# Decoding of w_out: sums of two or three blocks in one instruction, fewer steps per slot of attention, and another layout of the second stage's memory

## The chip, the cores and the metric

One core of a Trainium2 chip. Times are device microseconds of one execution. TensorE (PE) multiplies, VectorE (DVE) and ScalarE (ACT) work on elements, SyncE (SP) issues most transfers (DMAs); each engine works off its own instructions in program order and waits by semaphores. GpSimd (POOL) only clears a few constants.

## The reference

```python
def _attn_ref(q, k, v):                      # (8, 12, 448, 64)
    scores = scale * np.matmul(q, k.transpose(0, 1, 3, 2)) - np.log(S)
    attn = 1.0 / (1.0 + np.exp(-scores))
    return np.matmul(attn, v)

x = attn_out.transpose(0, 2, 1, 3).reshape(3584, 768)
h = x @ w_in                                 # w_in (768, 2048), float64 in memory
g = np.maximum(0.01 * h, h)
return g @ w_out                             # w_out (2048, 768), float64 in memory
```

The inputs q, k and v are float32; w_in and w_out come as 64-bit floats and are turned into 32-bit ones in the kernel.

## The kernel before

Every operand of a product is split into a rounded high part (made by ScalarE or VectorE) and a low part (x minus high, made by VectorE). Three matmuls (high x high, high x low, low x high) stand for one.

**Attention** runs in 24 rounds over pairs of heads, two pairs a round. A round has five slots: scores of the first pair, scores of the second, attention times v for the first and for the second, and a short ending. A slot's chores come ahead of its matmuls: copies of the results of the round before (`keep`, on VectorE for one of the two), the low parts of the next pairs' q and k (tile `qks`, slots 3 and 4), loads. **The first stage**, h = x w_in, is four passes of 56 slots (Strassen's scheme with 7 products, 18 matmuls a product, two slots each); it writes g, and sums of blocks of g, to memory. Low parts of w_in (tile `w`) are made three slots ahead of their use. **The second stage** is 52 products on two accumulators, lanes A and B, each product with one of 24 forms (sums of blocks) of w_out and a sum of blocks of g. Results collect in output tiles `o`.

**Decoding.** A generator, `prep`, decodes the weights step by step on VectorE, in 8 blocks of w_in, then 8 of w_out; a block comes in 4 pieces of 5 instructions (tile `wd`), and each `yield` ends a step. For a block of w_in, `firsts` makes four sums and stores; 9 empty steps (`WAIT`) follow. For a block of w_out, `second` makes sums of the 8 sub-blocks of 192 columns after the list `STEPS`: the first ones into a new tile `ws` (s0 to s7) and partly in place, then it stores both tiles ("store", to the memory tile `t`), then waits 9 empty steps, then makes more sums in place in `wd` (d0 to d7) and stores them. The sums behind the wait overwrite what is being stored, so the first of them also waits for that transfer itself.

In attention `prepare(pace, time)` is called after each slot. It adds the slot's pace to a credit and takes steps, one credit each, while the time counted for VectorE's instructions (0.14 us and a column's time for each) is below the slot's time:

```python
credit += pace
while credit >= 1 and queue < time - LESS:
    next(preps, None)
    credit -= 1
queue = max(0.0, queue - time)
```

In the first three passes of the first stage `fill` takes up to 4 steps a slot while the counted time is below 1.6 us of a slot's 1.8. `now` counts slots (3 before round 0); `ALONE` = 100 is the count from which decoded pieces are loaded ahead less far.

**Memory.** The tile pools on the left side lie one behind the other: `ring` (weights of the first stage, v), `stage` (their raw form), `l` tiles, then, after attention, `st` (results of the first stage) and `m` tiles; `l` and `m` hold the first stage's last operands. After the first stage the same addresses take `t2b` (weights of the second stage), `outp` (8 output tiles), `op` (8 more tiles for operands of the second stage). A tile's first use waits for the last use of what lay there. PSUM's 8 banks take `px` (banks 0 to 3) and `pz` (4 to 7) in the first stage, lane A (0 to 2), lane B (3 to 5) and two single banks `one` in the second; the last bank tiles of the first stage's last products are `px` (2, 3) and `pz` (6, 7).

All helper-issued instructions carry line 127 in the profile; read it by tile names.

Of the kernel before, what the change touches and what calls it, by code (L numbers as in the profile page):

```python
# [14 lines left out]
ALU = mybir.AluOpType  # L15
PSUM = bass.MemoryType.PSUM

P = 128
# [6 lines left out]
RING, STAGE = 4, 4  # L25
ST = 7
AHEAD, FAR, SPARE = 5, 6, 1
GG, OO, WW = 7, 8, (3, 3)
READY, LEAD = 2, 2

PACES = 5.5, 6.5, 5.5, 3.7, 2.7
TIMES = 1.92, 1.92, 2.33, 2.33, 1.66
PRODUCT, LESS, MOST = 1.8, 0.2, 4
WAIT = 9
ALONE = 100
LATER = 4
IDLE = 7
# [9 lines left out]


PRODUCTS = (
# [13 lines left out]
FORMS = 24  # L63
BLOCKS = "00", "01", "10", "11", "20", "21", "30", "31"
STEPS = (
# [7 lines left out]


def part(i):
# [14 lines left out]
def attn_ffn_kernel(ctx: ExitStack, tc: tile.TileContext, qk, v, w_in, w_out, out):  # L90
# [54 lines left out]
    def sub(to, x, y):  # L145
        vec(out=to, in0=x, in1=y, op=ALU.subtract)
# [21 lines left out]
        now += 1  # L168

    left, right = ExitStack(), ExitStack()  # L170
    ring = left.enter_context(tc.tile_pool(name="ring", bufs=RING))
    stage = left.enter_context(tc.tile_pool(name="stage", bufs=STAGE))

    prepared = set()

    class Weights:
# [17 lines left out]
    class Wide:  # L194
# [18 lines left out]
        def of(self, part, e, m):  # L213
            return self.t[:, part, e, m * P:m * P + P]
# [58 lines left out]
    def banks(name, sizes, stack=ps):  # L273

        pool = stack.enter_context(tc.tile_pool(name=name, bufs=1, space=PSUM, reuse_waits="tile"))

        def psum(tag, name):
            bufs, n = sizes[tag]
            return pool.tile([P, n, 512] if n > 1 else [P, 512], F32, tag=tag, name=name, bufs=bufs)

        return psum
# [50 lines left out]
    def firsts(u, dec):  # L332
# [7 lines left out]
            yield  # L340
        dma(out=to[:, 3:], in_=sums)

    def second(u, dec):


        n = len(BLOCKS)
        size = wide // 2
        e, at = u // 2, u % 2 * size
        both = {"d": dec.rearrange("p a b -> p (a b)").rearrange("p (n m) -> p n m", n=n),
                "s": block(F32, (n, size), f"ws1_{u}")}  # L350

        def of(x):
            return both[x[0]][:, int(x[1:])]

        for what, *x in STEPS:
            if what == "wait":
                yield from (None for _ in range(WAIT))
            elif what == "store":
                side, i, n, form = x
                dma(out=t2d[:, form:form + n, e, at:at + size], in_=both[side][:, i:i + n])  # L360
            else:
                to, a, x, b, y = x
                if a == b == -1:
                    vec_st(out=of(to), in0=of(x), scalar=-1.0, in1=of(y), op0=ALU.mult, op1=ALU.subtract)
                elif b == 1:
                    (add if a == 1 else sub)(of(to), of(y), of(x))
                else:
                    sub(of(to), of(x), of(y))
                yield

    def prep():

        n = 4
        pieces = [(m, k) for m in range(len(todo)) for k in range(n)]
        raws = []

        def load():
            at = len(raws)  # L380
            if at == len(pieces):
                return
            m, k = pieces[at]
            w, u = todo[m]
            size = 4 * HW // n
            pool = (stage, "stage", 2 * HW, STAGE) if at % 2 and now < ALONE else (pp, "wr", 2 * HW, 3)
            raw = block(I32, (size, 2), f"wr{w}_{u}_{k}", pool)
            dma(out=raw.rearrange("p m t -> p (m t)"), in_=(w_in, w_out)[w][u][:, k * size:(k + 1) * size].bitcast(I32))
            raws.append(raw)

        for _ in range(3):
            load()
        yield
        for at, (m, k) in enumerate(pieces):
            w, u = todo[m]
            if k == 0:
                dec = block(F32, (4, HW), f"wd{w}_{u}")
            raw = raws[at]
            size = 4 * HW // n
            low, high = raw[:, :, 0], raw[:, :, 1]  # L400
            tf = dec.rearrange("p b m -> p (b m)")[:, k * size:(k + 1) * size]
            t = tf.bitcast(I32)
            vec_s(out=t, in0=high, scalar1=0x7FFFFFFF, scalar2=None, op0=ALU.bitwise_and)
            yield
            vec_s(out=tf, in0=tf, scalar1=W_LEAST, scalar2=W_MOST, op0=ALU.max, op1=ALU.min)
            yield
            vec_s(out=t, in0=t, scalar1=5, scalar2=2, op0=ALU.logical_shift_left, op1=ALU.logical_shift_right)
            yield
            vec_st(out=t, in0=high, scalar=-0x40000000, in1=t, op0=ALU.bitwise_and, op1=ALU.bitwise_or)
            yield  # L410
            vec_st(out=t, in0=low, scalar=29, in1=t, op0=ALU.logical_shift_right, op1=ALU.bitwise_or)
            yield
            while len(raws) < min(at + 1 + (5 if now < ALONE else 3), len(pieces)):
                load()
            yield
            if k < n - 1:
                continue
            if w == 1:
                yield from second(u, dec)
            else:  # L420
                yield from firsts(u, dec)
            prepared.add((w, u))
            yield from (None for _ in range(WAIT))

    preps = prep()
    credit = 0.0
# [566 lines left out]

    assert {(1, u) for u in range(NU)} <= prepared
    t2b = ctx.enter_context(tc.tile_pool(name="t2b", bufs=WW[1], reuse_waits="tile"))
    outp = ctx.enter_context(tc.tile_pool(name="outp", bufs=OO, reuse_waits="tile"))
    shift(ctx, "pad3", 64)
    op = ctx.enter_context(tc.tile_pool(name="op", bufs=1, reuse_waits="tile"))
    spare.extend((op, f"o{n}") for n in range(8))
    cycle = [t2a] * WW[0] + [t2b] * WW[1]  # L1000
    weights += [Wide(k, cycle[k % len(cycle)]) for k in range(WW[0], total)]
    psum = banks("ps_o", dict(A=(1, 3), B=(1, 3), one=(2, 1)))
    NM = NC // 2
    ends = max(i for i, x in enumerate(PRODUCTS) if x[2] and x[1] == PRODUCTS[-1][1])
    outs, accs = {}, {}
# [30 lines left out]
    for k in range(total):  # L1036
# [3 lines left out]
        def work():  # L1040
# [13 lines left out]
                    x.low()  # L1054
            if begins:
                if p == NQ // 2 - 1 and i == ends:
                    t, one = psum(lane, f"acc_{lane}{k}"), psum("one", f"acc_one{k}")
                    accs[lane] = [t[:, 0, :S], t[:, 1, :S], one[:, :S]], [(slice(0, 2), t[:, :2, :S]), (slice(2, 3), one[:, None, :S])]
                else:
                    t = psum(lane, f"acc_{lane}{k}")  # L1060
                    accs[lane] = [t[:, m, :S] for m in range(3)], [(slice(0, 3), t[:, :, :S])]
# [67 lines left out]
```

## Time and profile before

| | |
|---|---|
| median of 3 runs | 1067.89 us (1066.1 to 1068.75) |
| the profiled execution | 1067.47 us, span 1065.7 us |
| attention, first stage, second stage | 0 to 277.8, to 681.5, to 1065.7 us of the span |
| busy: PE, DVE, ACT | 98%, 79%, 55% |
| mean granted TensorE clock | 0.990 |
| bytes moved | 300.63 MB, mean 282 GB/s |

The times of the engines overlap; the span is set by whichever work ends last. A row such as "PE sc <- DVE qks: 10.7, 3, 4.4" says that TensorE, about to write tile sc, waited for VectorE's writing of qks 10.7 us in all, 3 times, 4.4 at the longest. In rows of a group, "busy, mean ns" stands before the second bar and idle time of the engine just before, with its releaser, behind it. In a timeline the columns are start and length in us, engine, operation, tiles, and in brackets the idle time before it.

### The profile page before, as it was taken

Reading aid. Unit: us, or ns where it says so; the run is one execution under the profiler, and the core shown is the slowest. Engines: PE = TensorE matmul, PEld = TensorE weight load, DVE = VectorE, ACT = ScalarE, POOL = GpSimd, SP = SyncE. Lnnn points to the kernel's source line nnn. Section 1 sums busy time; section 2 is a strip of 40 time slices with the busy share of each in tenths; the row PEclk is TensorE's granted clock in tenths of the full one; section 3 lists DMA queues with packets and bytes.
Section 4 is the critical chain, followed back from the end, with each engine's and each line's share of the span. In section 5 each row is a group of like instructions: output and inputs, shape, how many; then the busy total and the mean of one; then the engine's idle time right before and its main releaser. Section 6 shows DMA issues by size and latency. Waiting matters only on the chain.

```text
span 1065.7 us, 15110 instructions
## 1 busy us (share of the span) xinstructions
PE 1039.8 (98%) x5738; PEld 868.3 (81%) x5738; DVE 845.8 (79%) x1024; ACT 585.0 (55%) x610; POOL 0.3 (0%) x5
## 2 busy tenths in 40 slices
PE   9999998888999999999999999999999999999997
PEld 5545554444799999999999999889999999999997
DVE  4889997667887879878865566599998888899883
ACT  6778786666554654555556545465444526444430
POOL 0000000000000000000000000000000000000000
PEclk9999999899899999999999999999999999999999
DMA  7998877778688798898986788898668698666923
GB/s 274 316 342 289 288 284 265 252 241 297 222 304 303 245 308 285 285 335 293 377 293 208 230 298 293 333 421 343 230 248 323 253 396 329 256 238 245 319 93 129
DMA packets 113336, 300.63 MB, mean 282 GB/s; under 512 B 9200, under 2 KB 51312, under 8 KB 113264
## 3 DMA queue, kind: packets, MB, share of 16 engines
q1 hardware_dynamic: 111248, 295.19, 77.7%
q10 hardware_dynamic: 2016, 4.47, 1.1%
q8 instruction: 45, 0.74, 0.3%
q14 instruction: 27, 0.22, 0.1%
HBM read 202.77 MB, written 96.86 MB: 281 GB/s over the span
## 4 chain that ended last, share of the span: by engine, by line
PE 88%; DMA 5%; DVE 4%; issue 1%; ACT 1%; SPq 0%; ACTq 0%; DVEq 0%
PE px_h L127 22%; PE acc_B L127 17%; PE acc_A L127 16%; PE pz_h L127 11%; PE pv L127 9%; PE sc L127 8%; PE py_h L127 5%; DMA t<-wd 2%; DVE wd L127 2%; DMA w<-t 1%; DVE ws L127 1%; DVE qks L127 1%; DMA wx<-t 1%; DMA wr<-in_w_out 1%; DVE x L127 0%
## 5 line engine op out<-in xcount | busy, mean ns | idle before, releaser
L127 PE MATMUL px_h<-hi,w 128*128 128x448 f32 x768 | 223.1, 361 | 0.0
L127 PE MATMUL acc_A<-gh,w 128*128 128x448 f32 x528 | 152.6, 363 | 1.0 <-ACT c_h L127 1.0
L127 PEld LDWEIGHTS px_h<-hi,w 128*128 128x128 f32 x768 | 143.9, 187 | 11.4 <-issue 0.7
L127 DVE TENSOR_TENSOR w<-wx,w 128x768 fp32r<-128x768 f32 x112 | 106.8, 954 | 53.2 <-ACT w L127 53.2
L127 PE MATMUL px_h<-lo,w 128*128 128x448 f32 x384 | 139.4, 363 | 0.0
L127 ACT ACTIVATE s<-sc 128x896 f32<-128x896 f32 x144 | 121.0, 932 | 29.9 <-PE sc L127 29.6
L127 PE MATMUL acc_B<-gh,w 128*128 128x448 f32 x424 | 123.0, 363 | 2.5 <-ACT o L127 1.5
L127 PE MATMUL sc<-qks 64*128 64x448 f32 (+1 forms) x876 | 105.7, 392 | 16.1 <-DVE qks L127 10.7
L127 PEld LDWEIGHTS sc<-qks 64*128 64x128 f32 x876 | 85.8, 202 | 43.5 <-issue 16.9
L127 PE MATMUL pv<-s,v 128*64 128x448 f32 x576 | 114.7, 547 | 0.0
L127 PE MATMUL pz_h<-hi,w 128*128 128x448 f32 x384 | 112.8, 362 | 0.0
L127 PEld LDWEIGHTS acc_A<-gh,w 128*128 128x128 f32 x528 | 99.1, 188 | 7.8 <-ACT c_h L127 1.4
L127 ACT ACTIVATE c_h<-c_h 128x896 f32<-128x896 f32 x48 | 45.8, 954 | 86.9 <-DVE c_h L127 86.9
L127 PEld LDWEIGHTS pv<-s,v 128*64 128x64 f32 x576 | 39.3, 138 | 64.9 <-issue 54.5
L127 ACT CAST w<-wx 128x768 fp32r<-128x768 f32 x112 | 91.3, 832 | 0.1
L127 DVE TENSOR_TENSOR w<-w 128x1536 fp32r<-128x1536 f32 x52 | 91.0, 1751 | 0.0
L127 PEld LDWEIGHTS acc_B<-gh,w 128*128 128x128 f32 x424 | 79.5, 188 | 8.7 <-ACT o L127 1.9
L127 PE MATMUL acc_B<-g,w 128*128 128x448 f32 x332 | 86.0, 361 | 0.0
L127 ACT CAST w<-w 128x1536 fp32r<-128x1536 f32 x52 | 76.9, 1478 | 0.7 <-DMA w<-t 0.7
L127 PEld LDWEIGHTS pz_h<-hi,w 128*128 128x128 f32 x384 | 71.9, 187 | 5.7 <-DVE w L127 0.3
L127 PEld LDWEIGHTS px_h<-lo,w 128*128 128x128 f32 x384 | 72.1, 188 | 3.8
L127 DVE SCALAR_TENSOR_TENSOR wd<-wr,wd 128x384 int32<-128x384 int32 x128 | 71.4, 558 | 3.5
(98 smaller groups left out, 1582.8 us busy)
## 6 DMA issues: line engine op xcount, KB each, us to landing
wx<-t SPq DMA_DIRECT2D x112, 384.0 KB, 4.9
w<-t SPq DMA_DIRECT2D x52, 768.0 KB, 4.4
g<-g SPq DMA_DIRECT2D x34, 896.0 KB, 7.2
g<-c_h SPq DMA_DIRECT2D x60, 448.0 KB, 4.5
g<-s SPq DMA_DIRECT2D x48, 448.0 KB, 5.5
qk<-in_qk SPq DMA_DIRECT2D x46, 448.0 KB, 5.4
g1s<-g SPq DMA_DIRECT2D x18, 896.0 KB, 6.6
wr<-in_w_in SPq DMA_DIRECT2D x32, 384.0 KB, 5.8
```

What stands on the lines that cost most here:

```text
L127: return lambda *args, **kw: tc.keep_in_program_order(issue(*args, **kw))
```

## The change

The steps granted per slot of attention go from 23.9 to 18.0 a round. The sums of w_out are written over runs of blocks with a start and a step, so that one instruction makes one, two or three of them: 12 instructions a block of w_out instead of 18, by another order of the sub-blocks and of the 24 forms; the forms are the same sums of blocks otherwise, and the list of products changes in the forms' numbers alone. From slot count 100 on, the empty wait is 4 steps instead of 9, and the empty step behind each piece goes. On the left side `stage` comes ahead of `ring` and `op` ahead of `outp`: t2b's first tile then lies over `stage`, six of the eight `op` tiles over `l` and two over the first four `st` tiles, the first two `outp` tiles over the last three `st` tiles and the others over `m`. In PSUM the lanes lie at: one0 in bank 0, B in 1 to 3, A in 4 to 6, one1 in 7. The last product's three columns go to one0, one1 and the first bank of B, three tiles, where before the first two shared B's tile.

```diff
-PACES = 5.5, 6.5, 5.5, 3.7, 2.7
+PACES = 4, 5, 4.2, 2.8, 2
...
-WAIT = 9
+WAIT, REST = 9, 4
...
 STEPS = (
-    ("sum", "s0", 1, "d1", -1, "d7"), ("sum", "s1", -1, "d2", 1, "d4"), ("sum", "s2", -1, "d2", -1, "d3"),
...
-    ("sum", "d3", 1, "d5", -1, "d6"), ("sum", "d1", -1, "d2", 1, "d1"), ("store", "d", 0, 8, 16))
+    ("sum", 3, "sub", ("s", 0, 1), ("d", 0, 1), ("d", 2, 1)),
+    ("sum", 1, "neg", ("s", 3, 1), ("d", 3, 1), ("d", 6, 1)),
+    ("sum", 2, "sub", ("s", 4, 1), ("d", 6, 0), ("s", 1, -1)),
+    ("sum", 1, "sub", ("s", 6, 1), ("s", 4, 1), ("d", 4, 1)),
+    ("sum", 1, "sub", ("s", 7, 1), ("s", 0, 1), ("s", 1, 1)),
+    ("sum", 1, "sub", ("d", 3, 1), ("d", 3, 1), ("d", 5, 1)),
+    ("sum", 1, "neg", ("d", 2, 1), ("d", 7, 1), ("d", 2, 1)), ("store", "s", 0, 8, 0), ("store", "d", 0, 8, 8),
+    ("wait",), ("sum", 1, "add", ("d", 4, 1), ("d", 2, 1), ("d", 4, 1)),
+    ("sum", 2, "neg", ("d", 7, -6), ("d", 3, -2), ("d", 7, -3)),
+    ("sum", 2, "add", ("d", 2, 1), ("d", 2, 1), ("d", 0, 6)),
+    ("sum", 1, "neg", ("d", 5, 1), ("d", 2, 1), ("d", 5, 1)),
+    ("sum", 2, "sub", ("d", 6, -6), ("d", 4, -4), ("d", 7, -4)), ("store", "d", 0, 8, 16))
...
+    stage = left.enter_context(tc.tile_pool(name="stage", bufs=STAGE))
     ring = left.enter_context(tc.tile_pool(name="ring", bufs=RING))
-    stage = left.enter_context(tc.tile_pool(name="stage", bufs=STAGE))
...
+    def rest():
+        return (None for _ in range(WAIT if now < ALONE else REST))
...
             if what == "wait":
-                yield from (None for _ in range(WAIT))
+                yield from rest()
...
-            yield
+            if now < ALONE:
+                yield
...
             prepared.add((w, u))
-            yield from (None for _ in range(WAIT))
+            yield from rest()
...
-    outp = ctx.enter_context(tc.tile_pool(name="outp", bufs=OO, reuse_waits="tile"))
     shift(ctx, "pad3", 64)
     op = ctx.enter_context(tc.tile_pool(name="op", bufs=1, reuse_waits="tile"))
+    outp = ctx.enter_context(tc.tile_pool(name="outp", bufs=OO, reuse_waits="tile"))
...
-    psum = banks("ps_o", dict(A=(1, 3), B=(1, 3), one=(2, 1)))
+    psum = banks("ps_o", dict(one0=(1, 1), B=(1, 3), A=(1, 3), one1=(1, 1)))
+    for x in ("one0", "B", "A", "one1"):
+        psum(x, f"first_{x}")
...
-                    t, one = psum(lane, f"acc_{lane}{k}"), psum("one", f"acc_one{k}")
-                    accs[lane] = [t[:, 0, :S], t[:, 1, :S], one[:, :S]], [(slice(0, 2), t[:, :2, :S]), (slice(2, 3), one[:, None, :S])]
+                    three = [psum(x, f"acc_{x}{k}") for x in ("one0", "one1", lane)]
+                    three[2] = three[2][:, 0]
+                    accs[lane] = [x[:, :S] for x in three], [(slice(m, m + 1), x[:, None, :S]) for m, x in enumerate(three)]
```

More of the change, by code (lines that the diff above doesn't have):

```diff
@@ L49 @@
 PRODUCTS = (
[9 rows of a table removed]
[9 rows of a table added]
     (0, "A", False, ("+<1", "-1s2"), ("-010", "+110")), (6, "B", False, ("+1s1",), ("-110!",)),
[3 rows of a table removed]
[3 rows of a table added]
 FORMS = 24
-BLOCKS = "00", "01", "10", "11", "20", "21", "30", "31"
+BLOCKS = "01", "20", "31", "10", "21", "00", "11", "30"
 STEPS = (
[7 rows of a table removed]
[12 rows of a table added]
 def part(i):
@@ L350, in second, with of @@
                 "s": block(F32, (n, size), f"ws1_{u}")}
-        def of(x):
-            return both[x[0]][:, int(x[1:])]
+        def of(n, side, at, step):
+            x = both[side]
+            if step == 0:
+                return x[:, at:at + 1].broadcast_to((P, n, size))
+            end = at + (n - 1) * step + (1 if step > 0 else -1)
+            return x[:, at:end if end >= 0 else None:step]
         for what, *x in STEPS:
             if what == "wait":
-                yield from (None for _ in range(WAIT))
+                yield from rest()
             elif what == "store":
@@ L361, in second @@
             else:
[L362 to L366, printed above, removed]
+                n, fn, *x = x
+                to, x, y = (of(n, *z) for z in x)
+                if fn == "neg":
+                    vec_st(out=to, in0=x, scalar=-1.0, in1=y, op0=ALU.mult, op1=ALU.subtract)
                 else:
-                    sub(of(to), of(x), of(y))
+                    (add if fn == "add" else sub)(to, x, y)
                 yield
```

29 rows, old and new, of tables (PRODUCTS, STEPS) are left out of this document.

## The prediction

> **What bounds the kernel now.** I read the page first, then who waited for whom on TensorE and VectorE, then busy time by stretch, then the timeline at each long wait.
>
> ```profile
> span 1065.7 us, 15110 instructions
> ...
> PE 1039.8 (98%) x5738; PEld 868.3 (81%) x5738; DVE 845.8 (79%) x1024; ACT 585.0 (55%) x610; POOL 0.3 (0%) x5
> ```
>
> TensorE is busy 98% of the span, so a change that leaves its matmuls alone can win the 26 us in which it stands still, and time in which its clock is low. TensorE's waits:
>
> ```profile
> PE sc L127 <- DVE qks L127: 10.7, 3, 4.4
> PE sc L127 <- DVE x L127: 4.9, 3, 4.3
> PE acc_B L127 <- ACT o L127: 1.5, 1, 1.5
> ...
> PE acc_A L127 <- ACT c_h L127: 1.0, 1, 1.0
> PE acc_B L127 <- DVE o L127: 0.8, 1, 0.8
> PE acc_B L127 <- DVE w L127: 0.2, 1, 0.2
> ```
>
> 15.6 us fall on the scores (sc), in attention, where VectorE is late with the operands' lower parts (qks) or with the copy of a result (x). The long waits of VectorE itself from 168 to 278 us say why:
>
> ```profile
> DVE wd L127 <- DMA t<-wd: 27.0, 4, 7.7
> ```
>
> Four times, 27.0 us in all, it waits until a decoded block of w_out (wd) has been stored, because the next sum overwrites it. Rounds of attention, first a quiet one (columns: stretch, length, busy PE, PEld, DVE, ACT, POOL, clock, DMA):
>
> ```profile
> 171.84:182.00 10.16, 10.16 (x80) 5.44 (x76) 4.97 (x13) 7.84 (x11) 0.00 (x0) 1.00 0.63 203
> 182.00:198.19 16.19, 13.23 (x82) 7.33 (x78) 13.21 (x29) 8.23 (x11) 0.00 (x0) 0.79 0.71 237
> ...
> 208.34:223.84 15.50, 12.00 (x81) 6.45 (x78) 12.58 (x28) 8.19 (x11) 0.00 (x0) 0.89 0.68 221
> ...
> 234.01:250.75 16.74, 12.18 (x80) 6.50 (x76) 12.67 (x28) 8.18 (x11) 0.00 (x0) 0.90 0.64 211
> 250.75:261.41 10.66, 10.45 (x81) 5.37 (x77) 6.68 (x18) 7.86 (x11) 0.00 (x0) 1.00 0.98 359
> 261.41:277.82 16.41, 12.07 (x73) 6.41 (x69) 10.02 (x23) 7.46 (x10) 0.00 (x0) 0.79 0.83 266
> ```
>
> A quiet round takes 10.16 us. The last five rows exceed it by 6.03, 5.34, 6.58, 0.50 and 6.25: 24.7 us lost. About 15 of it is standing still; the rest is a lower clock (0.79 to 0.90) afterwards, 13.23 - 10.16 = 3.1, 1.8, 2.0 and 1.9 us, 2.2 on average. The first stall in detail:
>
> ```profile
> 172.59 0.62 DVE L127 COPY x<-pv 128x448 f32<-128x448 f32 x1 [0.56 <-ACT x L127]
> ...
> 177.40 0.47 SPq L127 DMA_DIRECT2D t<-wd  x1
> ...
> 182.00 0.47 PE L127 MATMUL sc<-qks 64*128 64x448 f32 x2
> ...
> 184.08 0.36 DVE L127 TENSOR_TENSOR wd<-wd 128x192 f32<-128x192 f32 x1 [6.71 <-DMA t<-wd]
> 184.35 1.02 DVE L127 TENSOR_TENSOR qks<-qk,qks 128x832 fp32r<-128x832 f32 x1
> ...
> 185.43 2.98 PE L127 MATMUL sc<-qks 64*128 64x448 f32 x14 [2.96 <-DVE qks L127]
> ```
>
> From the round's start at 171.84: store issued at +5.56, sum released at +12.24 (6.7 us), one sum, the lower part, TensorE on again at +13.59. It had run dry at +10.63. The code has an empty wait of 9 steps between store and sum, yet nothing of VectorE lies there.
>
> **Why the wait was empty, and the pacing.** A slot may take whole credits of steps while the counted VectorE time stays below the slot's; an empty step costs a credit but no time. Rows for the price of a step:
>
> ```profile
> L127 DVE SCALAR_TENSOR_TENSOR wd<-wr,wd 128x384 int32<-128x384 int32 x128 | 71.4, 558 | 3.5
> ...
> L127 DVE TENSOR_SCALAR wd<-wd 128x384 f32<-128x384 f32 x64 | 23.0, 359 | 1.8
> ...
> L127 DVE TENSOR_TENSOR wd<-wd 128x192 f32<-128x192 f32 x48 | 16.5, 352 | 32.9 <-DMA t<-wd 32.7
> ...
> L127 DVE TENSOR_TENSOR ws<-wd 128x384 f32<-128x384 f32 x16 | 8.9, 553 | 0.0
> ```
>
> Six steps of a piece (three of 0.36, two of 0.56, one empty) are 2.2 us, 0.36 a step. Before, 23.9 steps a round would be 8.6 us, with 2 x 1.02 for lower parts and 0.62 for the copy 11.3, more than the 10.16 of a round: steps are put off and credit piles up, and the 9 empty steps go by in one slot. After, 18.0 steps are 6.5, with the same 2.7 gives 9.2: credit is nearly used up and an empty step is worth its share of a slot. Counted through slot by slot with the code's own costs, 36 credits are left over in round 16 before, and 0 to 7 in any round after. But the change also cuts the wait to 4 steps from slot 100 on. w_in takes 8 x (24 + 4 + 9) = 296 steps; the first block of w_out stores after 24 + 7 more, at step 328. At 18 a round from round 1 this is 18 rounds and 4 steps: round 19, slot 1, which is slot count 3 + 95 + 2 = 100, exactly where the wait is 4. That slot has 6 credits: 4 empty steps and two sums. So the store still has nothing of VectorE behind it. A block is 20 + 7 + 4 + 5 + 4 = 40 steps from there: stores at step 368 (round 21, slot 2, with the steps that busy slots put off; 3 empty steps and two sums in the same slot) and 408 (round 23, slot 2). Three stalls in attention instead of four, earlier in their rounds; five blocks instead of four are left for the first stage.
>
> **Their price.** Three more places of the trace serve here: another store with its release, in the first stage; a shorter halt of TensorE; the clock after the first stall.
>
> ```profile
> 449.80 0.37 SPq L127 DMA_DIRECT2D t<-wd  x1
> ...
> 454.76 0.36 DVE L127 TENSOR_TENSOR wd<-wd 128x192 f32<-128x192 f32 x1 [1.66 <-DMA t<-wd]
> 455.04 0.62 DVE L127 SCALAR_TENSOR_TENSOR wd<-wd 128x192 f32<-128x192 f32 x2
> ```
> ```profile
> 703.18 1.48 ACT L127 CAST w<-w 128x1536 fp32r<-128x1536 f32 x1 [0.40 <-DMA w<-t]
> ...
> 704.57 1.27 ACT L127 COPY o<-acc_B 128x1344 f32<-128x1344 f32 x1
> ...
> 705.89 0.47 PE L127 MATMUL acc_B<-gh,w 128*128 128x448 f32 x1 [1.50 <-ACT o L127]
> ```
> ```profile
> 681.50:1060.50 379.00, 375.52 (x1873) 350.62 (x1872) 320.52 (x186) 170.80 (x116) 0.00 (x0) 1.00 0.73 274
> ```
> ```profile
> 186.00:188.00 2.00, 2.00 (x14) 1.77 (x12) 1.93 (x5) 0.92 (x1) 0.00 (x0) 0.50 0.03 8
> ```
>
> The store's data are the same, so I keep 6.7 us from issue to release in attention. VectorE starts a round with the copy, done at +1.37 by the row at 172.59. Two sums in a row take 0.62 (455.04), so each adds 0.27, and one of two blocks 0.27 + 0.20 = 0.47 (0.55 against 0.35). Round 19: four sums after the copy, store at +2.5, released +9.2, five sums 1.95, lower part 1.02: TensorE goes on at +12.2 and ran dry at +10.6, 1.6 lost. Round 21: a decode step and six sums, store at +4.4, released +11.1, two sums 0.74, lower part: +12.9, 2.2 lost (2.3 by rounding). Round 23: five decode steps and all seven sums, store at +6.2, released +12.9, a sum, and the lower part of the next stage's first weight (some 0.9): +14.1, needed at +10.6, 3.5 lost. Together 7.3. The clock: 2.96 us of standing still brought it to 0.50, the 1.50 us at 705.89 did not lower it, in a stretch at 1.00. So nothing for 1.6, half of 2.2 for the second, 2.2 for the third: 3.3. Attention then loses 10.6 against 24.7: **-14.1 us**. Bounds: released after 5.0 (the row at 454.76) the three lose 0, 0.5 and 1.8, a gain of 22; released 7.7 after, 2.6, 3.2 and 4.5 with 2.2 of clock each time, a gain of 8.
>
> The Trainium skill, "TensorE: Matmul & The Clock Gate", section "Why this matters for your kernels", asks for no idle gaps above about 3 us, or the clock falls to half. The trace agrees on the fall but shows it at 2.96; by the page the second stall too would keep the clock, and the sum would be 1.1 us lower.
>
> **The merged sums.** 18 instructions a block become 12, 48 fewer. By the rows two of 352 become one of 553, at most 0.15 x 48 = 7 us of VectorE, as chained 0.07 x 48 = 3, none of it on TensorE's path: 0.
>
> **First stage.** Five blocks store there, with a wait of 4 steps, about one slot of 1.8 us, where four stored before with 9. One of those, and what TensorE lost before the largest group of its matmuls there:
>
> ```profile
> 297.62 0.35 DVE L127 SCALAR_TENSOR_TENSOR wd<-wd 128x192 f32<-128x192 f32 x1
> ...
> 301.19 0.58 SPq L127 DMA_DIRECT2D t<-wd  x1
> ...
> 308.19 0.36 DVE L127 TENSOR_TENSOR wd<-wd 128x192 f32<-128x192 f32 x1 [1.01 <-DMA t<-wd]
> ```
> ```profile
> L127 PE MATMUL px_h<-hi,w 128*128 128x448 f32 x768 | 223.1, 361 | 0.0
> ```
>
> Release came 5.0 to 7.0 us after the issue, and once the store itself waited 3.6 on SP's queue. With 1 to 3 us of VectorE's work between, waits of 2 to 6 us follow, five times. Weights' lower parts are made three slots, 5.4 us, ahead, and waits of 1.01 and 1.66 cost TensorE 0.0. I take two of the five, where sums of results crowd in behind, at 1.5 us: **+3.0** (0 to 8). Behind a waiting sum stand those lower parts, and ScalarE's activations wait for VectorE's sums of results, then TensorE for ScalarE's copies. The fifth block's decoding, some 15 us of VectorE, lies in three passes of 100.8 us: 0.
>
> **Second stage.** Two more rows from its start (the casts, the copy and the wait at 703 to 706 stand above):
>
> ```profile
> 682.51 0.47 PE L127 MATMUL acc_A<-gh,w 128*128 128x448 f32 x1 [1.01 <-ACT c_h L127]
> ```
> ```profile
> 670.13 20.69 SPq L127 DMA_DIRECT2D g<-g  x3
> ...
> 691.86 1.65 SPq L127 DMA_DIRECT2D w<-t  x3
> ```
>
> Accumulator A now lies over banks that the last product doesn't write: -1.0. SP's queue stands until about 690.8 before a load whose tile lies over results still being stored, and of the weights queued behind it the second lands at 703; ScalarE's copy comes behind their cast, and TensorE waits 1.50 and 0.20. The operand tiles now lie over the first stage's operands, free when TensorE ends the stage at 681.5, so the weights land earlier: -1.7. In exchange two output tiles lie over those late results, and copies at about 690 may wait: +0.7 (0 to 2.7). Together **-2.0**, bounds -2.7 and 0. By the Trainium skill, "DMA: Bandwidth & Descriptors", section "Queues, rings and completion order", an engine alternates between queues, so SP's earlier loads would slow the stores on ScalarE's queue; no run shows it yet, and the sum by it would lie 1 or 2 us higher.
>
> **The end.** The last product's three columns get tiles of their own, so the second doesn't wait for the reading of the first: **-0.8** (the wait for DVE o above), bounds 0 and -0.8.
>
> **Sum.** -14.1 + 3.0 - 2.0 - 0.8 = -13.9. The profiled execution took 1067.47 us at a span of 1065.7, 0.4 below the median of 1067.89: 1067.5 - 13.9 = 1053.6.
>
> **Rivals.** (B) The stores are released before the sums come, because fewer decoding loads share the DMA engines: 24.7 won, 1067.5 - 24.7 + 3.0 - 2.8 = 1043. For it: release after 5.0 in the first stage; against: 27.0 us in 4 waits in attention. 15%. (C) Three stalls of the old size, 6.05 us on average: 18.2 lost, 6.5 won, 1067.5 - 6.5 + 3.0 - 2.8 = 1061.2. For it: the stalls won't shrink if other loads delay the earlier stores; against: the place in the round. 18%. (D) Slower: in the first stage the wait of 4 steps leaves VectorE standing 5 to 7 us at all five stores, beyond the 5.4 of lead, and TensorE loses 3.2 and a low clock's 2.2 each time: 27, net 27 - 16.9 = +10, 1077.6. It decides from 3.4 us a store on. Against: 0.0 idle on px_h so far. 6%. (E) The credits don't matter and the stalls stay in number and size: 1067.5 + 3.0 - 2.8 = 1067.7. 6%.
>
> **Numbers.** (A), the forecast, has 55%. Range 1040 to 1064: A with its bounds, B and C, 88%. A measurement here tells 0.3%, 3.2 us, from no change: faster is A, B, C (0.88), the same is E (0.06), slower D (0.06).
>
> **What would show it.** VectorE's waits for the store of wd: three in attention, in rounds 19, 21, 23, five in the first stage, TensorE's waits for qks down to one or two below 3 us, one wait of px_h or its weights at the start of the first stage, none of acc_A for c_h, none of acc_B for o at the end. Wrong if stores in attention have VectorE's work behind them, or if px_h shows idle time of several us from 330 to 560 us.

## The result, and the profile after

The change makes the kernel slower: 1074.34 us (median, 1073.51 to 1074.84) against 1066.99 us for the kernel before, run beside it; ratio 1.0068, 95% interval 1.0048 to 1.0088. The forecast was 1053.6. The profiled execution took 1073.51 us at a span of 1071.7. From its page:

```profile
PE 1039.7 (97%) x5738; PEld 870.3 (81%) x5738; DVE 842.2 (79%) x976; ACT 583.7 (54%) x610; POOL 0.3 (0%) x5
```

Who waited for whom on TensorE, in the changed kernel:

```profile
PE sc L132 <- DVE qks L132: 7.6, 2, 6.3
PE px_h L132 <- DVE c_h L132: 6.6, 2, 4.5
PE px_h L132 <- DVE w L132: 5.4, 2, 4.6
PE acc_B L132 <- ACT o L132: 4.9, 1, 4.9
```

The waits in attention (sc) are halved (15.6 to 7.9 us), those of acc_A for c_h and of acc_B for VectorE's o are gone. New are 12 us on px_h, in the first stage, and acc_B's wait for ScalarE's o grows from 1.5 to 4.9. By stretch (length; busy PE, PEld, DVE, ACT, POOL; clock; DMA share; GB/s), attention, first stage and second stage, each begun at the first matmul of the next; the kernel before, then the changed one:

```profile
0.00:277.80 277.80, 260.63 (x1850) 139.93 (x1850) 215.72 (x447) 193.68 (x243) 0.30 (x5) 0.96 0.82 283
277.80:682.50 404.70, 403.71 (x2020) 377.76 (x2016) 308.93 (x390) 221.42 (x252) 0.00 (x0) 1.00 0.83 289
682.50:1065.70 383.20, 375.51 (x1872) 350.62 (x1872) 321.20 (x188) 169.88 (x115) 0.00 (x0) 1.00 0.73 274
```
```profile
0.00:259.90 259.90, 250.94 (x1850) 135.45 (x1850) 193.98 (x373) 192.27 (x243) 0.31 (x5) 0.99 0.82 276
259.90:682.90 423.00, 410.74 (x2021) 382.22 (x2018) 326.92 (x415) 220.50 (x251) 0.00 (x0) 0.98 0.85 293
682.90:1071.70 388.80, 378.04 (x1873) 352.63 (x1871) 321.28 (x188) 170.92 (x116) 0.00 (x0) 0.99 0.72 270
```

Attention wins 17.9 us, the first stage loses 18.3, the second 5.6. In the first stage 11.3 of the 18.3 are standing still (length less PE busy: 12.3 against 1.0), 7.0 are longer matmuls, that is, a lower clock. The 1.0 of the kernel before is its wait for c_h, just ahead of the border at 682.5; the prediction counts that wait to the second stage (from 681.5 on), and so does the table further down.

**Attention.** VectorE's wait for the store of wd from 168 to 285 us, then where TensorE stood still behind it, the clock behind the third stall, and the store of round 21 with its release:

```profile
DVE wd L132 <- DMA t<-wd: 23.8, 3, 10.5
```
```profile
211.69 1.88 PE L132 MATMUL sc<-qks 64*128 64x448 f32 x16 [1.27 <-DVE qks L132]
...
239.17 5.02 PE L132 MATMUL sc<-qks 64*128 64x448 f32 x34 [6.35 <-DVE qks L132]
265.23 1.11 PE L132 MATMUL px_h<-hi,w 128*128 128x448 f32 x2 [4.62 <-DVE w L132]
```
```profile
262.70:269.50 6.80, 4.27 (x12) 3.82 (x13) 5.52 (x9) 0.00 (x0) 0.00 (x0) 0.51 0.57 199
```
```profile
227.10 1.00 SPq L132 DMA_DIRECT2D t<-wd  x1
```
```profile
237.23 0.36 DVE L132 TENSOR_TENSOR wd<-wd 128x192 f32<-128x192 f32 x1 [10.49 <-DMA t<-wd]
```

Three stalls instead of four, in rounds 19, 21 and 23, as forecast. But the second release comes 10.1 us after its store's issue, not 6.7; and the third stall (4.62, and half clock from 262.7 to 269.5) lies behind the border at 259.9, so that the stretches above book it to the first stage.

Not all of the 17.9 us is won at the stalls. At the start of the round in which the stalls of the kernel before begin (171.84, shown in the prediction) the changed kernel is already 2.6 us ahead, and 1.7 of that stems from the first 18 us of the span. The same matmuls, the kernel before first:

```profile
18.49 3.91 PE L127 MATMUL sc<-qks 64*128 64x448 f32 x36
```
```profile
16.79 3.91 PE L132 MATMUL sc<-qks 64*128 64x448 f32 x36
169.29 3.91 PE L132 MATMUL sc<-qks 64*128 64x448 f32 x36
```

The kernel with the PSUM change alone (experiment 2), whose attention is that of the kernel before, is at this matmul at 16.16. The 1.7 us are therefore no effect of the change, but of this one execution of the kernel before; why it was late there is not shown.

**First stage.** The two places that cost most (VectorE, ScalarE, TensorE), and the clock behind them:

```profile
475.33 0.36 DVE L132 TENSOR_TENSOR wd<-wd 128x192 f32<-128x192 f32 x1 [5.94 <-DMA t<-wd]
...
492.00 1.09 DVE L132 TENSOR_TENSOR s<-s,c_h 128x896 f32<-128x896 f32 x1 [4.91 <-DMA g<-s]
```
```profile
496.46 0.95 ACT L132 ACTIVATE c_h<-c_h 128x896 f32<-128x896 f32 x1 [6.49 <-DVE c_h L132]
```
```profile
496.57 0.71 PE L132 MATMUL px_h<-hi,w 128*128 128x448 f32 x1 [4.50 <-DVE c_h L132]
```
```profile
549.51 0.36 DVE L132 TENSOR_TENSOR wd<-wd 128x192 f32<-128x192 f32 x1 [4.58 <-DMA t<-wd]
...
551.61 0.44 PE L132 MATMUL px_h<-hi,w 128*128 128x448 f32 x1 [2.14 <-DVE c_h L132]
```
```profile
494.80:501.70 6.90, 5.13 (x15) 4.62 (x15) 6.90 (x8) 2.62 (x3) 0.00 (x0) 0.52 0.97 317
552.90:556.30 3.40, 3.40 (x12) 3.03 (x11) 2.51 (x4) 1.22 (x2) 0.00 (x0) 0.54 0.55 173
```

At 549.5 the wait for the block's store alone makes VectorE late. At 492 it is a second store: a result's save (g<-s) that the next sum in place must let go first. The kernel before waits for this save too, and loses nothing by it:

```profile
496.61 1.09 DVE L127 TENSOR_TENSOR s<-s,c_h 128x896 f32<-128x896 f32 x1 [3.18 <-DMA g<-s]
```

There the save landed 3.9 us after its issue, and VectorE went on 4.7 us before TensorE needed px_h (at 501.34). Here the save took 5.7 us, VectorE had come to these sums 2.5 us later against TensorE's need, and it went on only 0.1 before that need (at 492.07). That VectorE came late because of the wait of 5.94 ahead of it fits, but is not shown (experiment 3).

**Second stage.** ScalarE's last four saves of the first stage, and what waits for them, with the clock behind it and VectorE's wait; then the landing of those saves (last column: median us from issue to landing), the kernel before first:

```profile
685.15 3.46 ACTq L132 DMA_DIRECT2D g<-s  x4
...
693.76 3.65 ACT L132 COPY o<-acc_A 128x1344 f32<-128x1344 f32 x3 [1.81 <-DMA g<-s]
704.21 1.69 ACT L132 CAST g1s<-gf 128x1792 fp32r<-128x1792 f32 x1 [6.81 <-DVE gf L132]
...
709.87 0.74 PE L132 MATMUL acc_B<-gh,w 128*128 128x448 f32 x1 [4.94 <-ACT o L132]
```
```profile
709.90:716.70 6.80, 6.17 (x16) 5.03 (x17) 6.80 (x5) 3.06 (x2) 0.00 (x0) 0.52 1.01 414
```
```profile
700.09 2.03 DVE L132 TENSOR_TENSOR gf<-g,g 128x1792 f32<-128x1792 f32 x1 [5.75 <-DMA g<-s]
```
```profile
g<-s ACTq DMA_DIRECT2D x4, 448.0 KB, 3.7
```
```profile
g<-s ACTq DMA_DIRECT2D x4, 448.0 KB, 8.6
```

VectorE's gf, whose tile is one of the two that now lie over results still being saved, stands 5.75 us until 700.09; ScalarE's cast stands 6.81 behind it, its copy of acc_B comes late, and TensorE stands 4.94, again with half clock (0.52 from 709.9 to 716.7).

### The profile page after: what moved, and what is told of

It is laid out like the page before. It is cut to its first block, busy times and chain, and to the rows that moved or that the text cites. A ratio compares the mean times of both kernels' runs of the same rounds, so it can differ in the third digit from the quotient of the medians.

```text
span 1071.7 us, 15049 instructions
## 1 busy us (share of the span) xinstructions
PE 1039.7 (97%) x5738; PEld 870.3 (81%) x5738; DVE 842.2 (79%) x976; ACT 583.7 (54%) x610; POOL 0.3 (0%) x5
## 4 chain that ended last, share of the span: by engine, by line
PE 85%; DVE 6%; DMA 6%; issue 1%; ACT 1%; SPq 0%; ACTq 0%; DVEq 0%
PE px_h L132 19%; PE acc_B L132 17%; PE acc_A L132 16%; PE pv L132 10%; PE sc L132 9%; PE pz_h L132 8%; PE py_h L132 5%; DMA t<-wd 3%; DMA g<-s 2%; DVE wd L132 2%; DMA wx<-t 1%; DVE w L132 1%; DVE s L132 1%; DVE c_h L132 1%; DVE gf L132 1%
## 5 line engine op out<-in xcount | busy, mean ns | idle before, releaser
L132 PE MATMUL px_h<-hi,w 128*128 128x448 f32 x768 | 229.0, 369 | 12.3 <-DVE c_h L132 6.6
L132 PEld LDWEIGHTS px_h<-hi,w 128*128 128x128 f32 x768 | 146.9, 192 | 25.8 <-issue 8.5
L132 ACT ACTIVATE s<-sc 128x896 f32<-128x896 f32 x144 | 119.7, 932 | 18.3 <-PE sc L132 18.3
L132 PEld LDWEIGHTS sc<-qks 64*128 64x128 f32 x876 | 81.6, 190 | 32.0 <-issue 16.9
L132 PE MATMUL sc<-qks 64*128 64x448 f32 (+1 forms) x876 | 97.7, 373 | 7.9 <-DVE qks L132 7.6
```

The lines of the kernel that those rows point to most:

```text
L132: return lambda *args, **kw: tc.keep_in_program_order(issue(*args, **kw))
```

## The experiments

All ratios are to the kernel before, run beside each; below 1 is faster. "Second stage" is the length of that stretch in the profiled execution, "landing" the median landing of ScalarE's four last saves there.

**1. Layout, as a whole.** The changed kernel with the old layout, and the kernel before with the new one.

The first edit is this, with the tiles of the last product (not printed here) put back too; the second is its reverse:

```diff
-    stage = left.enter_context(tc.tile_pool(name="stage", bufs=STAGE))
     ring = left.enter_context(tc.tile_pool(name="ring", bufs=RING))
+    stage = left.enter_context(tc.tile_pool(name="stage", bufs=STAGE))
...
+    outp = ctx.enter_context(tc.tile_pool(name="outp", bufs=OO, reuse_waits="tile"))
     shift(ctx, "pad3", 64)
     op = ctx.enter_context(tc.tile_pool(name="op", bufs=1, reuse_waits="tile"))
-    outp = ctx.enter_context(tc.tile_pool(name="outp", bufs=OO, reuse_waits="tile"))
...
-    psum = banks("ps_o", dict(one0=(1, 1), B=(1, 3), A=(1, 3), one1=(1, 1)))
+    psum = banks("ps_o", dict(A=(1, 3), B=(1, 3), one=(2, 1)))
```

> The changed kernel with the memory of the second stage as it was before: order of the pools ring and stage, op and outp, the three PSUM lanes, and the two tiles of the last band. Theory 1 (the saves of g on ScalarE's queue land late because SP's loads of the second stage's weights now start 5 us sooner, and PE stands behind them): the second stage goes back from 388.8 us to some 384 to 385, the median landing of the saves at 685 to 690 us from 8.6 us to about 4, PE's wait for acc_B behind ScalarE's o (4.9 us) is gone, a wait of 1 us for c_h comes back; about 1069.5 us in all, 4 to 5 us below the changed kernel. Rival (the layout is not to blame, the later start of the second stage is): 1073 to 1077 us, landing still near 8 us.

Measured: 1068.88 us, ratio 1.0024 (1.0013 to 1.0034); second stage 382.5 us, landing 2.9.

> The kernel before with the four changes of layout alone, its decoding as it was. Theory 1: the second stage grows by 4 to 5 us as in the changed kernel, 1071 to 1072 us in all, with the landing of the last saves at 8 us or more and a wait of PE for acc_B near 700 us. Rival (the late saves come from the decoding's later end): the layout brings the 2 to 2.8 us that the prediction gave it, 1064 to 1065 us.

Measured: 1069.91 us, 1.0038 (1.0024 to 1.0053); second stage 388.0 us, landing 8.6, TensorE's wait for acc_B 5.0 us. By the ratios the layout costs 4.7 us with the new decoding and 4.1 with the old (5.5 and 3.2 by the medians); the late saves come with it in both.

**2. Which part of the layout.** First on the kernel of experiment 3 (1055.5 us): of the edit above, only the two lines of stage and ring, then only those of outp and op.

> The kernel with a wait of nine steps in the first stage too (1055.5 us), with the pools ring and stage in the order of before; op and outp stay in the new order. Theory 1 says the late saves have one cause, SP's loads of the second stage's weights that start sooner because ring lies where its buffers come free sooner: with the old order the loads start some 5 us later, the saves land in about 4 us, ScalarE's o and VectorE's gf no longer wait for them; the second stage goes from 386.5 us to 382 or 383, 1051 to 1052 us in all. Rival (the loads' start does not matter, but that op lies over tiles which the saves still read): 1055 us.

> The same kernel with op and outp in the order of before; ring and stage stay in the new order. Theory 1: the loads still start sooner and the saves still land in 8 us or more, but no tile of op lies over a tile that a late save reads, so VectorE's and ScalarE's waits for the saves move to whatever else needs them or go; 1052 to 1055 us. Rival (op's place alone is to blame): the second stage back to 382 or 383 us with the saves still late, 1051 us.

Measured: ring and stage back, 1055.42 us (0.9897, 0.9879 to 0.9915), second stage 388.2 us; op and outp back, 1053.33 us (0.9871, 0.9847 to 0.9894), second stage 382.7 us (in an execution of 1050.07). The theory had the wrong pool. ScalarE's queue with the saves, and SP's first load behind them, with the new and with the old order of op:

```profile
668.18 3.45 ACTq L132 DMA_DIRECT2D g<-s  x4
668.65 0.32 SPq L132 DMA_DIRECT2D g<-g  x1
```
```profile
667.83 3.46 ACTq L132 DMA_DIRECT2D g<-s  x4
674.03 0.32 SPq L132 DMA_DIRECT2D g<-g  x1
```

With op in its new place the loads start at 668.65, while ScalarE's queue issues the saves (668.2 to 671.6), and these land in 8.6 us; in its old place they start when the saves are through, which land in 2.9. So the second rival was right that op's place alone is to blame, and wrong that the saves would stay late without it. The swap does two things at once, it moves the loads and it lays op's tiles over the results being saved; which share each has was not tried apart. Then the changed kernel with op and outp alone put back:

> The changed kernel with one thing undone: the order of op and outp as it was before; ring and stage, the PSUM lanes, the sums and the decoding as changed. The theory formed from the two runs with one pool order each (the whole loss of the second stage comes from the place of op): the saves of g land in about 3 us at the median, VectorE's gf and ScalarE's o no longer wait for them, the second stage goes from 388.8 to 382 or 383 us; 1068 to 1069 us in all. Rival (in the changed kernel, where the saves start later, the order of ring and stage matters too): 1071 us or more, landing 6 us or more.

Measured: 1068.64 us, 1.0025 (1.0013 to 1.0037), second stage 382.5 us, landing 2.9: as good as the whole old layout. The order of op and outp is all that the layout lost. And the PSUM part, the last line of the edit with the three end tiles, on the kernel before:

> The kernel before with the new PSUM lanes and the three tiles of the last band alone. The prediction's own terms for this part, the wait of 1 us for c_h at the second stage's start and of 0.8 us for VectorE's o at the end: 1.8 us less, 1064 to 1066 us, with no wait of acc_A for c_h and none of acc_B for VectorE's o. Rival (what is late next, ScalarE's o, takes the place): no difference from the kernel before.

Measured: 1067.22 us, 1.0006 (0.9995 to 1.0018): no gain. Its longest wait of TensorE from 676 to 720 us:

```profile
PE acc_B L127 <- ACT o L127: 2.1, 1, 2.1
```

The waits of 1.0 and 0.8 are gone, but TensorE arrives earlier at ScalarE's o, waits 2.1 instead of 1.5, and this halt drops the clock (last section).

**3. The wait of four steps.** The changed kernel with nine steps between store and sums throughout, and no rest at a block's end from slot count 100 on.

```diff
             if what == "wait":
-                yield from rest()
+                yield from (None for _ in range(WAIT))
-WAIT, REST = 9, 4
+WAIT, REST = 9, 0
```

> The changed kernel with a wait of nine steps between a block's store and its second sums in the first stage too (four before), and no rest at a block's end there. Theory 1 (the wait of four steps is too short for the store and VectorE stands in it, which PE feels at 478 and 552 us): VectorE's waits for the store between 285 and 580 us fall from 19.2 us to 6 to 9, PE's two waits for px_h of 4.5 and 2.1 us and the two stretches of half clock behind them go, 1063 to 1067 us in all. Rival (VectorE's standing there is covered by work made ahead, and the first stage lost its time elsewhere): within 2 us of the changed kernel's 1074.

Measured: 1055.46 us, 0.9901 (0.9886 to 0.9916): 18.9 below the changed kernel (17.8 by the ratios), more than expected. Slot count 100 lies in round 19, so the wait of four steps also held in attention's last rounds. The stalls there now cost little:

```profile
PE sc L132 <- DVE x L132: 3.1, 2, 1.6
PE sc L132 <- DVE qks L132: 1.0, 1, 1.0
PE pz_h L132 <- DVE w L132: 0.8, 1, 0.8
```

By stretch it wins 4.9 us in attention, 10.7 in the first stage (the stall behind the border and the one at 551 are gone) and 2.3 in the second. The wait for the save of s stays, with 9.0 us on VectorE and 5.3 on TensorE. Here VectorE is not late, it comes to these sums 12.5 us before TensorE's need (8.8 in the changed kernel, 11.3 in the kernel before), but the save takes 9.3 us to land. So a late landing is enough for this stall; what the four steps cost at 492, and why the same save lands after 3.9, 5.7 or 9.3 us, is not shown.

**4. The merged sums alone**, on the kernel before.

> The kernel before with the merged sums, their new order of blocks and the renumbered forms alone; steps per slot, the wait of nine steps and the layout as before. Merged sums leave fewer steps, so decoding gets ahead, and the stores of the blocks come at other slots. Theory 1 (a sum of two or three blocks takes as long as its parts, so that merging is free by itself, and only where the stores and their waits fall matters): attention keeps four or five waits of VectorE for the store of wd; within 4 us of the kernel before, 1063 to 1071 us. Rival (merged operands cost more, or hold longer stretches of VectorE against the queue of its other work): over 1072 us, with more PE waits for qks, x and px_h without a store ahead of them.

Measured: 1073.6 us, 1.0069 (1.0052 to 1.0086), outside the range of theory 1 and in the rival's, yet not by the rival's mechanism: each long wait has a store ahead of it. VectorE's waits for the store from 168 to 300 us:

```profile
DVE wd L132 <- DMA t<-wd: 38.2, 5, 9.7
```

Five stalls instead of four. Fewer steps a block move the stores to other slots; two of them now land in 9.5 and 9.6 us, where none took more than 7.6 before.

**5. The wait counted in slots.** The kernel before with merged sums and the new PSUM tiles; between store and sums a number of slots must pass, so that credit cannot use the wait up at once. The nine empty steps at the end of a block of w_out go as well. The edit to the kernel before, with the numbers of the second run; the first has five and four slots, the third seven and five:

```diff
+    def rest():
+        until = now + (6 if now < 123 else 5)
+        while now < until:
+            yield
...
             if what == "wait":
-                yield from (None for _ in range(WAIT))
+                yield from rest()
...
-            yield from (None for _ in range(WAIT))
+            yield from (None for _ in range(WAIT * (w == 0)))
```

> The kernel before with the merged sums and the new PSUM lanes and last tiles, its pools, and the steps per slot of attention as before; the wait between a block's stores and its second sums is no longer counted in steps but in slots: five slots of attention or four of the first stage must pass, and there is no rest at the end of a block of w_out. Theory 1 (each stall of VectorE is the store's own landing less the work issued in between, and nothing else): VectorE's waits for the store fall below 2 us each, PE's waits for qks, x and px_h below 1.5 us, no half clock near 185 to 270 us; the first matmul of px_h at 252 to 256 us, the first stage 404 to 408 us, the second 381 to 383; 1040 to 1046 us in all. Rival (the same stalls only move, since later sums pile up in the slots behind the wait): 1052 us or more.

Measured: 1046.43 us, 0.9812 (0.9794 to 0.9831), just above the expected range: VectorE's waits for the store are 0.8 us in all, but the wait for the save of s is still there, 7.2 us on VectorE and 3.7 on TensorE, and the first stage takes 411.1 us.

> As the run before, with a wait of six slots in attention and five in the first stage. Theory 1: where the landing takes 10 us (two of the four stores in attention with merged sums), six slots cover it and five do not, so the last small waits go too; 0 to 3 us below the run with five and four, 1039 to 1045 us, with decoding that ends some 10 slots of the first stage later. Rival (sums pile up): 1052 us or more.

Measured: 1041.07 us, 0.9767 (0.9747 to 0.9787), faster than both kernels. Its first two stretches:

```profile
0.00:251.20 251.20, 249.32 (x1850) 134.23 (x1850) 197.27 (x380) 192.08 (x243) 0.31 (x5) 1.00 0.84 290
251.20:656.80 405.60, 404.13 (x2021) 377.90 (x2018) 323.89 (x408) 220.77 (x251) 0.00 (x0) 1.00 0.87 303
```

Attention without stalls lasts 251 us at a clock of 1.00.

> The fastest kernel so far (six and five slots, 1041.1 us) with seven slots in attention. Theory 1: its stores in attention land 6.0 to 6.6 us after their issue and six slots cover that already, so there is nothing more to be had: 1039 to 1043 us; later stores may fall into the first stage and bring one wait of VectorE more there. Rival (longer is better still): under 1038 us.

Measured: 1040.60 us, 0.9762 (0.9741 to 0.9782): nothing more to be had there, as expected.

> The kernel before with its sums one by one, its layout and its steps per slot; only the wait between a block's stores and its second sums is counted in slots, four in attention and four in the first stage, with no rest at a block's end of w_out (five and six do not let the decoding end in time with sums one by one). Theory 1 (the wait counted in slots is what brings the gain, merging only makes room for it): VectorE's waits for the store fall to 0 to 3 us each where the landing takes 6 to 8 us, attention ends at 253 to 258 us; 1043 to 1050 us in all. Rival (merging itself brings part of it): attention ends after 262 us, 1055 us or more.

Measured: 1045.09 us, 0.9797 (0.9777 to 0.9817), attention 250.1 us. With the 18 sums one by one, the old layout and the old pacing, the wait in slots, with the rest at a block's end gone, brings 21 of the 25 us; these two were not tried apart. Of the other 4, the longer waits, the sums and the PSUM tiles were not told apart. The smaller paces by themselves were not tried.

## Why the prediction was wrong, point by point

It missed by 19.9 us in the profiled executions. The terms of the sum, set against the stretches. The third stall is counted to attention (4.6 of standing, and 2.1 of clock: half of the 4.27 busy in 262.7 to 269.5), and the wait of 1.0 for c_h to the second stage:

| term | forecast | measured |
|---|---|---|
| attention, from 171.84 (before) to the end of its third stall | -14.1 | -8.6 |
| attention ahead of its stalls | 0 | -2.6 |
| merged sums | 0 | no cost by themselves |
| first stage | +3.0 | 19.3 - 6.7 = +12.6 |
| second stage and end | -2.8 | +4.6 |

The steps that failed are the price of the first stage's waits (9.6 of the miss), the second stage, which had the wrong sign (7.4), and the release time in attention (5.5).

- **Attention**: number, rounds and mechanism were right (the wait used up in one slot, so nothing of VectorE behind the store). Mis-sized was the release, kept at 6.7 us "since the store's data are the same": it came after 6.0, 10.1 and 7.2. TensorE stood 12.5 us in all (1.27 and 0.25, 6.35, 4.62) where 7.3 was forecast. The bound of 7.7 did not hold: the same bytes landed after 5.9, 10.0 and 7.1 us in these three rounds, and why is not shown. The term for the clock came out well, some 3.6 (half of the 3.03 and 4.27 busy behind the second and third stall) against 3.3. With 8.6 won the term lies just inside its bounds of 8 to 22. That the whole stretch comes out at 11.2 is in part luck: 2.6 of it were won ahead of the stalls, and 1.7 of these the kernel before lost in its first 18 us, which the change does not touch.
- **Merged sums**: right by themselves (VectorE's busy time fell by 3.6 us, attention in experiment 5 is as short with as without). That a merge moves every later store was counted under attention; with the old steps per slot and waits this move alone costs 6.9 us (experiment 4).
- **First stage**: this step failed. The waits for the stores came as forecast, five of them, 19.2 us in all and 5.9 at the longest, but two at 1.5 us each, without clock, was the wrong price. The one at 549.5 cost TensorE 2.14 and 1.7 of clock (half of 3.40). The largest loss, 4.50 and 2.6 of clock (half of 5.13) at 496.6, came behind a wait for the save of s, for which the prediction has no term. Two small waits add 1.0: together 11.9 of the 12.6. The cover of 5.4 us for low parts of weights held but for 0.8; that VectorE's own sums of results have no such cover was named and not priced. Rival D, with 6%, had halts of TensorE with a low clock here, but by another path (low parts made too late), at all five stores and with 27 us.
- **Second stage**: wrong in sign. I gave op's new place 1.7 us for earlier loads, and 0.7 against it for copies that might wait. The loads did start earlier, and that was the harm: they ran beside the saves, which two of op's tiles and two output tiles wait for. The Trainium skill, "DMA: Bandwidth & Descriptors", section "Queues, rings and completion order", says that a DMA engine goes round between the queues that have work; landing of 8.6 against 2.9 us with and without SP's loads beside it agrees. I had put 1 or 2 us on it; op's place costs some 5 us (4.6 by the ratios of the changed kernel and its variant with op put back, 5.7 by the medians, experiment 2).
- **PSUM and end** (-1.8): the waits went, as forecast, and the gain with them, to ScalarE's o (experiment 2, 1.0006). The row of 1.5 us that stands next was quoted, and not asked what is late next.

What was to show the prediction wrong did: px_h idle for several us between 330 and 560 us. TensorE's wait of 6.3 us for qks, where none above 3 was forecast, did so for the release.

## What to carry to other kernels

A wait in a generator that is there to let a transfer land must be counted in time that passes (slots of the bottleneck), not in its own steps, or the steps it saves up are spent on it at once: with the rest at a block's end gone too, this was worth some 20 us. An earlier load is a gain only if nothing that someone waits for is on the way at that moment; check which stores are still out where a tile's address changes. And price a short halt of TensorE with the clock behind it, not alone: here, half of one or two times 3.41 us.

## What the runs showed of the hardware

The same halt may or may not cost the clock. TensorE's matmul behind ScalarE's o, and two stretches around it (columns as above), in the kernel with the PSUM change alone and in the one with nine steps and op back:

```profile
704.21 0.47 PE L127 MATMUL acc_B<-gh,w 128*128 128x448 f32 x1 [2.11 <-ACT o L127]
```
```profile
701.48:704.89 3.41, 1.30 (x6) 0.53 (x4) 3.41 (x2) 3.38 (x3) 0.00 (x0) 1.00 1.02 420
704.89:708.31 3.42, 3.21 (x9) 2.87 (x10) 3.42 (x3) 2.22 (x2) 0.00 (x0) 0.50 1.02 419
```
```profile
689.51 0.47 PE L132 MATMUL acc_B<-gh,w 128*128 128x448 f32 x1 [2.19 <-ACT o L132]
```
```profile
685.63:689.04 3.41, 1.70 (x9) 1.24 (x7) 3.41 (x3) 3.02 (x3) 0.00 (x0) 1.00 1.02 423
689.04:692.46 3.42, 2.73 (x12) 2.24 (x13) 3.42 (x3) 3.40 (x3) 0.00 (x0) 1.00 1.01 417
```

2.11 us of standing still brought 0.50, 2.19 did not; 2.14 at 551.6 did, 1.27 at 211.7 did not. The borders of the stretches shown here explain it. Eleven of the fourteen traces have stretches at half clock, and in each of them all its starts and ends (78 together) lie within 0.01 us on a grid of 3.413 us, whose offset differs from execution to execution. On this grid the clock of a stretch follows from the stretch before it. The eleven agree: where TensorE stood 1.76 us or less in a stretch at full clock, the next one had full clock too, and where it stood 2.06 or more, the next one ran at half; in between lie 1.83, 1.85 and 1.86 us with half and one 1.86 with full. A stretch at half clock was the last one where TensorE stood at most 0.60 us in it, and another followed from 0.66 on. So the halt of 2.11 us, which lies whole in one stretch, drops the clock, and the halt of 2.19, of which 1.71 lie in one stretch and the rest in the next, does not. How long a halt may be is thus a matter of where it falls. The limit of about 3 us that the Trainium skill gives ("TensorE: Matmul & The Clock Gate", section "Why this matters for your kernels") is not safe here.
